# Sink set-up by DMA, start-up constants and the place of VectorE's last sum in a windowed-attention and highway kernel

## The chip, the cores and the metric

The kernel runs on one NeuronCore of one Trainium2 chip. A core has five engines that run side by side and meet only at semaphores: TensorE (PE; its weight loads are shown as PEld), VectorE (DVE), ScalarE (ACT), GpSimd (POOL) and SyncE (SP). Transfers between the chip's memory and the core's working memory (SBUF) run on 16 DMA engines; they are issued from GpSimd's queue and from SP's. TensorE writes its results to a second memory, PSUM. The metric is the device time of one launch in microseconds (us); lower is better.

## The reference

```python
scores = scale * np.matmul(q, k.transpose(0, 1, 3, 2))
is_sink = pos[None, :] < int(n_sink)
rel = pos[:, None] - pos[None, :]
in_window = (rel >= 0) & (rel < int(window))
scores = np.where(is_sink | in_window, scores, -1000000000.0)
scores = scores - np.max(scores, axis=-1, keepdims=True)
a = np.exp(scores)
a = a / (np.sum(a, axis=-1, keepdims=True) + 1e-09)
attn = np.matmul(a, v)
x = attn.transpose(0, 2, 1, 3).reshape(B * S, H * D)
Hh = np.maximum(x @ w_h, 0.0)
T = 1.0 / (1.0 + np.exp(-(x @ w_t + b_t)))
out = T * Hh + (1.0 - T) * x
```

q, k and v are (4, 8, 768, 64) in float32: 4 batches, 8 heads, 768 positions, 64 values a head. A query sees the 128 positions up to its own (the window) and the first 4 positions of its batch (the sink). The attention output, 3072 rows of 512, goes through a highway layer with two 512 x 512 weights.

## The kernel before

The 3072 rows are 24 blocks of 128 (NB = 24), six to a batch (NSC = 6). Block n = 6b + c is block c of batch b. With a window of 128, a block needs its own keys and those of the block before it; from c = 2 on it needs the sink as well.

One main loop (line 335) runs over i and works on several blocks at a time. In the pass of i it calls, in this order:

- `stage_sink(i)` for two blocks at once, where c is 2 or 4: scores of the sink keys (sk, L222) and their exponentials (es, L225).
- `stage_S(i+1)`: scores (sps, L242) and their exponentials on ScalarE (e, L245), in two halves.
- `stage_A(i)`: probabilities times values (av, L273), from c = 2 on also the sink's part (L279); then on VectorE the reciprocal of the row sums (rec, L286) and the scaled output (xh, L288).
- `stage_T(i+2)`: transposes of q and k into one PSUM tile (tp, L182 and L184), copied by ScalarE (qT, L187) and VectorE (kT, L188).
- `load` and `load_v` of block i+10 (q, k and v, cast to half precision on the way; L84, L85 and L92).
- `stage_mask(i+1)` on VectorE (L258).
- `stage_Mt(i-1)`: the first weight (tps, L307 and L309) and tanh on ScalarE (u, L312).
- `stage_X(i)`: xh transposed (xtp, L297) and copied by ScalarE (xT, L299).
- `stage_sink_setup` where c = 0: VectorE copies the batch's four sink keys into a block-diagonal tile (ks, L198); TensorE spreads the sink values over the partitions by a matmul with a selection matrix (vps, L203); VectorE multiplies the result by a block mask (vs, L207).
- `stage_Mh(i-1)`: the second weight (hps, L321), then on VectorE dd (L324), ee (L327) and otok (L330), and the output transfer from SP (L332).

The sigmoid is done as a tanh. The exponentials carry a common factor of 1.9, and the values have a column of 2.0 behind each head's 64 values, so that rec comes out of the same matmul as the output.

What sets the order: inside `manual_schedule` each engine that is named issues its instructions in the order in which the program emits them. In the main loop those are TensorE, VectorE and ScalarE; GpSimd and SP are placed there by the planner. A first region (line 106) names GpSimd alone and holds the first loads, the two weights and the making of `ident`, `mask` and `bdm`. How the instructions of one region fall among those of the same engine outside it is the planner's choice.

PSUM: tp, sk, tps and hps share one ring of two buffers (`m_ps`), so each of them waits until the tile two places earlier has been read. av, vps and xtp share a single buffer (`av_ps`). The scores have two (`s_ps`).

SBUF: eight buffers each for q and k as loaded, a ring of 11 tiles for v (`v_ring`), all of them set to 2.0 in full on VectorE before the first load (L104). All constants are written ahead of the main loop: `mask0` and `mask1` (L141 to L145), the bias row (L151, L155), `sel` (L159, L161) and the zeroed ks tiles (L167).

Of the kernel before, what the change touches and what calls it, by code (L numbers as in the profile page):

```python
# [21 lines left out]
def kernel(  # L22
# [18 lines left out]
    nc = tc.nc  # L41
# [25 lines left out]
    r_pool = ctx.enter_context(tc.tile_pool(name="p_r", bufs=3))  # L67
    x_pool = ctx.enter_context(tc.tile_pool(name="p_x", bufs=4))
    td_pool = ctx.enter_context(tc.tile_pool(name="p_td", bufs=3))
# [23 lines left out]


    ebias = const.tile([P, 1], FP32, tag="ebias")
    nc.vector.memset(ebias, _EXP_BIAS)
    wh_sb = const.tile([P, NOC, DM], FP16, tag="wh")
    wt_sb = const.tile([P, NOC, DM], FP16, tag="wt")
    ident = const.tile([P, P], FP16, tag="ident")
    mask = const.tile([P, 2, P], FP16, tag="mask", name="mask")  # L100
    nc.vector.memset(ident, 1.0)
    nc.vector.memset(mask, 1.0)
    for vt in v_ring:
        nc.vector.memset(vt, 2.0)  # L104

    with tc.manual_schedule(engines={ENG.Pool}):
        load(0)
        nc.gpsimd.affine_select(
            out=ident, in_=ident, compare_op=ALU.is_equal, fill=0.0,
            base=0, pattern=[[-1, P]], channel_multiplier=1)  # L110
        load_v(0)
        load(1)

        nc.gpsimd.affine_select(
            out=mask[:, 1, :], in_=mask[:, 1, :], compare_op=ALU.is_ge, fill=0.0,
            base=0, pattern=[[1, P]], channel_multiplier=-1)
# [8 lines left out]
        nc.gpsimd.dma_start(out=wh_sb, in_=moe_w_h.rearrange("(kc p) of -> p kc of", p=P))  # L125
        load_v(3)
        bdm = const.tile([P, H], FP32, tag="bdm")
        nc.gpsimd.memset(bdm, 1.0)
        bdm3 = bdm.rearrange("p (a b) -> p a b", b=2)
        nc.gpsimd.affine_select(  # L130
            out=bdm3, in_=bdm3, compare_op=ALU.is_ge, fill=0.0,
            base=0, pattern=[[-32, NHP], [-4, 2]], channel_multiplier=1)
        nc.gpsimd.affine_select(
            out=bdm3, in_=bdm3, compare_op=ALU.is_ge, fill=0.0,
            base=NSINK - 1, pattern=[[32, NHP], [4, 2]], channel_multiplier=-1)
        for n in range(4, AHEAD):
            load(n)
            load_v(n)

    mask0 = const.tile([P, P], FP16, tag="mask0", name="mask0")  # L140
    nc.vector.tensor_copy(out=mask0, in_=mask[:, 1, :])  # L141
    nc.vector.memset(mask0[0:NSINK, :], 1.0)
    mask1 = const.tile([P, 2, P], FP16, tag="mask1", name="mask1")
    nc.vector.tensor_copy(out=mask1, in_=mask)
    nc.vector.memset(mask1[0:NSINK, 0, :], 1.0)  # L145

# [7 lines left out]
    nc.vector.memset(ones_row[0:1, :], 1.0)  # L154
    nc.vector.tensor_scalar_mul(bt16[0:1, :], bt32, 0.5)  # L155


    sel = const.tile([P, NHP, 32], FP16, tag="sel")
    nc.vector.memset(sel, 0.0)  # L159
    for hh in range(2):  # L160
        nc.vector.tensor_copy(  # L161
            out=sel[:, :, 4 * hh:4 * hh + NSINK],
            in_=ident[:, 0:NSINK].unsqueeze(1).to_broadcast([P, NHP, NSINK]))
    ks_bd = []
    for i in range(2):
        t = const.tile([P, NHP * 160], FP16, tag=f"ks{i}", name=f"ks{i}")
        nc.vector.memset(t, 0.0)  # L167
        ks_bd.append(t)


    qkT = {}
    e_of = {}
    es_of = {}
    vs_of = {}
    xh_of = {}
    xT_of = {}

    def stage_T(n):
# [7 lines left out]
        kT = qkT_pool.tile([P, NHP, P], FP16, tag="kT", name="kT")  # L186
        nc.scalar.copy(out=qT, in_=tp[:, 0:NHP, :])  # L187
        nc.vector.tensor_copy(out=kT, in_=tp[:, NHP:2 * NHP, :])  # L188
        qkT[n] = (qT, kT)

    def stage_sink_setup(b):

        _, kT = qkT[b * NSC]
        ks = ks_bd[b % 2]
        ks3 = ks.rearrange("p (a b) -> p a b", b=160)
        for hh in range(2):
            rows = slice(64 * hh, 64 * hh + 64)
            nc.vector.tensor_copy(out=ks3[rows, :, 4 * hh:4 * hh + NSINK],  # L198
                                  in_=kT[rows, :, 0:NSINK])
# [5 lines left out]
        vs = es_pool.tile([P, 2, 4, 65], FP16, tag="vs", name="vs")  # L205
        for g in range(2):
            nc.vector.tensor_tensor(  # L207
                out=vs[:, g, :, :],
                in0=vps[:, g, 0:260].rearrange("p (h e) -> p h e", e=65),
                in1=bdm[:, 4 * g:4 * g + 4].unsqueeze(2).to_broadcast([P, 4, 65]),  # L210
                op=ALU.mult)
        vs_of[b] = vs

# [48 lines left out]
    def stage_A(n):  # L262
# [4 lines left out]
        for g in range(2):  # L267
# [10 lines left out]
            if c >= 2:  # L278
                nc.tensor.matmul(  # L279
                    av[:, g, :, 0:65], lhsT=es_of[n][:, c % 2, :],  # L280
                    rhs=vs_of[b][:, g, :, :], start=False, stop=True,
                    skip_group_check=True)
# [3 lines left out]
        nc.vector.reciprocal(out=rec.unsqueeze(2), in_=avh[:, :, 64:65])  # L286
        xh = x_pool.tile([P, H, D], FP16, tag="xh", name="xh")
        nc.vector.tensor_tensor(  # L288
# [26 lines left out]
    def stage_Mh(n):  # L315
        xT = xT_of.pop(n)
        xh = xh_of.pop(n).rearrange("p h d -> p (h d)")
# [9 lines left out]
        nc.vector.scalar_tensor_tensor(out=ee, in0=u, scalar=1.0, in1=dd,  # L327
                                       op0=ALU.add, op1=ALU.mult)
        otok = o_pool.tile([P, DM], FP32, tag="otok", name="otok")
        nc.vector.scalar_tensor_tensor(out=otok, in0=xh, scalar=2.0, in1=ee,  # L330
# [3 lines left out]
    with tc.manual_schedule(engines={ENG.PE, ENG.DVE, ENG.Activation}):  # L334
        for i in range(-2, NB + 1):
            s = i + 1
# [15 lines left out]
            if 0 <= i < NB:  # L352
                stage_X(i)
            if 0 <= i < NB and i % NSC == 0:
                stage_sink_setup(i // NSC)
            if 0 <= i - 1 < NB:
# [36 lines left out]
```

## Time and profile before

| what | us |
|---|---|
| median of 13 runs | 140.56 |
| lowest and highest run | 140.0 and 141.48 |
| the profiled execution | 141.32 |
| its span | 139.6 |
| busy in the span: TensorE, VectorE | 114.6, 117.3 |
| busy in the span: ScalarE, GpSimd | 90.5, 66.2 |
| first transposes of q and of k start | 5.0 and 6.64 |
| first scores (L242) start | 10.75 |
| last otok (L330) starts | 135.56 |

The page has the span in 40 equal slices; each digit is the busy share of a slice in tenths, and PEclk is the clock that TensorE was granted:

```profile
PE   0206779989999889999999699999996999999730
DVE  6895466769988999899898999898989998999590
ACT  3015961868776957987867497778768678874310
POOL 6999776599987988886748260000000000000000
PEclk9999999999999999999999999999999999999995
```

In a timeline row stand the start, the time taken, the engine, the line, the operation, the tile written and the tiles read, the shapes and the count; in brackets the engine's idle time ahead of it and what ended that. An engine with a letter q behind it (SPq) is that engine's queue.

### The profile page before, as it was taken

Reading aid. Unit: us, or ns where it says so; the run is one execution under the profiler, and the core shown is the slowest. Engines: PE = TensorE matmul, PEld = TensorE weight load, DVE = VectorE, ACT = ScalarE, POOL = GpSimd, SP = SyncE. Lnnn points to the kernel's source line nnn. Section 1 sums busy time; section 2 is a strip of 40 time slices with the busy share of each in tenths; the row PEclk is TensorE's granted clock in tenths of the full one; section 3 lists DMA queues with packets and bytes.
Section 4 is the critical chain, followed back from the end, with each engine's and each line's share of the span. In section 5 each row is a group of like instructions: output and inputs, shape, how many; then the busy total and the mean of one; then the engine's idle time right before and its main releaser. Section 6 shows DMA issues by size and latency. Waiting matters only on the chain.

```text
span 139.6 us, 3303 instructions
## 1 busy us (share of the span) xinstructions
PE 114.6 (82%) x1312; PEld 74.0 (53%) x1312; DVE 117.3 (84%) x235; ACT 90.5 (65%) x129; POOL 66.2 (47%) x84
## 2 busy tenths in 40 slices
PE   0206779989999889999999699999996999999730
PEld 0105656646754464766565367657653665675300
DVE  6895466769988999899898999898989998999590
ACT  3015961868776957987867497778768678874310
POOL 6999776599987988886748260000000000000000
PEclk9999999999999999999999999999999999999995
DMA  0999999999999999999999969221011021101111
GB/s 7 108 128 127 159 186 161 151 183 155 189 185 168 202 198 158 200 200 189 190 147 148 186 52 162 84 77 73 6 75 75 0 80 75 60 20 75 75 75 75
DMA packets 79408, 16.98 MB, mean 122 GB/s; under 512 B 75297, under 2 KB 76321, under 8 KB 79394
## 3 DMA queue, kind: packets, MB, share of 16 engines
q0 software_dynamic: 75936, 10.49, 111.8%
q1 hardware_dynamic: 3458, 6.30, 12.4%
q8 instruction: 10, 0.16, 0.5%
q14 instruction: 4, 0.03, 0.1%
HBM read 20.97 MB, written 6.29 MB: 195 GB/s over the span
## 4 chain that ended last, share of the span: by engine, by line
DVE 33%; PE 29%; DMA 13%; ACT 9%; issue 7%; POOL 6%; DVEq 0%; POOLq 0%
PE hps L321 11%; DMA ksd<-in_k_dram 7%; DVE ee L327 6%; DVE otok L330 6%; DMA wt_sb<-in_moe_w_t_dram 6%; DVE dd L324 6%; ACT e L245 6%; DVE e L258 5%; DVE xh L288 5%; PE tps L309 4%; PE xtp L297 3%; PE av L273 3%; DVE kT L188 3%; POOL qsd L84 3%; PE sk L222 2%
## 5 line engine op out<-in xcount | busy, mean ns | idle before, releaser
L245 ACT ACTIVATE e<-sps,ebias 128x1024 f16<-128x1024 f32 (+1 forms) x48 | 47.4, 1039 | 17.0 <-PE sps L242 13.0
L258 DVE TENSOR_TENSOR e<-e,mask 128x1024 f16<-128x1024 f16 (+1 forms) x48 | 28.7, 638 | 0.0
L92 POOL DMA_DIRECT2D v<-in_v_dram x24 | 21.6, 903 | 8.6 <-PE tp L182 5.8
L309 PE MATMUL tps<-wt_sb,xT 128*128 128x512 f16 x96 | 25.3, 388 | 0.0
L273 PE MATMUL av<-v,e 128*128 128x112 f16 x352 | 24.5, 219 | 0.7 <-DVE vs L207 0.7
L321 PE MATMUL hps<-wh_sb,xT 128*128 128x512 f16 x96 | 24.6, 378 | 0.6
L84 POOL DMA_DIRECT2D qsd<-in_q_dram x24 | 21.5, 896 | 6.9 <-DMA wt_sb<-in_moe_w_t_dram 1.5
L273 PEld LDWEIGHTS <-e 128*128 128x128 f16 x352 | 20.4, 100 | 4.0 <-DVE vs L207 1.0
L85 POOL DMA_DIRECT2D ksd<-in_k_dram x24 | 21.4, 892 | 2.0 <-DMA wh_sb<-in_moe_w_h_dram 1.2
L312 ACT ACTIVATE u<-tps 128x512 f16<-128x512 f32 x24 | 14.4, 600 | 9.6 <-PE tps L309 9.6
L324 DVE SCALAR_TENSOR_TENSOR dd<-hps,xh 128x512 f16<-128x512 f32 x24 | 16.5, 688 | 3.7 <-PE hps L321 3.7
L187 ACT COPY qT<-tp 128x512 f16<-128x512 f16 x24 | 14.0, 585 | 8.5 <-PE tp L184 8.5
L242 PE MATMUL sps<-qT,kT 64*128 64x128 f16 x352 | 15.2, 227 | 4.3 <-DVE kT L188 3.7
L327 DVE SCALAR_TENSOR_TENSOR ee<-u,dd 128x512 f16<-128x512 f16 x24 | 16.6, 692 | 2.5
L330 DVE SCALAR_TENSOR_TENSOR otok<-xh,ee 128x512 f32<-128x512 f16 x24 | 16.6, 692 | 0.8
L288 DVE TENSOR_TENSOR xh<-av,rec 128x512 f16<-128x512 f32 x24 | 16.6, 692 | 0.8
L242 PEld LDWEIGHTS <-kT 64*128 64x128 f16 x352 | 10.7, 98 | 11.7 <-issue 6.8
L188 DVE COPY kT<-tp 128x512 f16<-128x512 f16 x24 | 10.0, 419 | 6.2 <-ACT qT L187 6.2
L299 ACT COPY xT<-xtp 128x512 f16<-128x512 f16 x24 | 14.0, 582 | 1.4 <-PE xtp L297 0.9
L182 PE MATMUL tp<-ident,qsd 128*128 128x128 f16 x96 | 10.2, 235 | 5.2 <-DMA qsd<-in_q_dram 5.2
L309 PEld LDWEIGHTS <-xT 128*128 128x128 f16 x96 | 9.6, 100 | 9.1 <-issue 0.8
L297 PEld LDWEIGHTS <-xh 128*128 128x128 f16 x96 | 6.2, 100 | 13.6 <-DVE xh L288 11.5
(45 smaller groups left out, 107.0 us busy)
## 6 DMA issues: line engine op xcount, KB each, us to landing
out_dram<-otok SPq DMA_DIRECT2D x24, 256.0 KB, 3.0
qsd<-in_q_dram POOLq DMA_DIRECT2D x24, 128.0 KB, 6.9
ksd<-in_k_dram POOLq DMA_DIRECT2D x24, 128.0 KB, 7.0
v<-in_v_dram POOLq DMA_DIRECT2D x24, 128.0 KB, 7.5
wt_sb<-in_moe_w_t_dram POOLq DMA_DIRECT2D x1, 512.0 KB, 8.2
wh_sb<-in_moe_w_h_dram POOLq DMA_DIRECT2D x1, 512.0 KB, 9.9
bt<-in_moe_b_t_dram SPq DMA_DIRECT2D x1, 2.0 KB
```

What stands on the lines that cost most here:

```text
L84: nc.gpsimd.dma_start(out=qsd, in_=q[b, :, rows, :].transpose([1, 0, 2]))
L92: nc.gpsimd.dma_start(out=vt[:, :, 0:D], in_=v[b, :, rows, :].transpose([1, 0, 2]))
L242: nc.tensor.matmul(sps[:, hh, o:o + P], lhsT=kk[rows, hp, :], rhs=qT[rows, hp, :], start=True, stop=True)
L245: nc.scalar.activation(out=e.rearrange("p a b c d -> p a (b c d)"), in_=sps[:, :, 0:2 * np_ * P], func=AF.Exp, bias=ebias, scale=SCALE)
L258: nc.vector.tensor_tensor(out=ev, in0=ev, in1=m.unsqueeze(1).to_broadcast([P, 4, np_ * P]), op=ALU.mult)
L273: nc.tensor.matmul(av[:, g, 2 * hl + hh, 0:_AVN], lhsT=es[g][:, hh, hl, pc, :], rhs=vt[:, 65 * h:65 * h + _AVN], start=first, stop=False, ...
L288: nc.vector.tensor_tensor(out=xh, in0=avh[:, :, 0:D], in1=rec.unsqueeze(2).to_broadcast([P, H, D]), op=ALU.mult)
L309: nc.tensor.matmul(tps, lhsT=xT[:, kc, :], rhs=wt_sb[:, kc, :], start=False, stop=(kc == NOC - 1))
L321: nc.tensor.matmul(hps, lhsT=xT[:, kc, :], rhs=wh_sb[:, kc, :], start=(kc == 0), stop=(kc == NOC - 1))
L324: nc.vector.scalar_tensor_tensor(out=dd, in0=hps, scalar=0.0, in1=xh, op0=ALU.max, op1=ALU.subtract)
L327: nc.vector.scalar_tensor_tensor(out=ee, in0=u, scalar=1.0, in1=dd, op0=ALU.add, op1=ALU.mult)
L330: nc.vector.scalar_tensor_tensor(out=otok, in0=xh, scalar=2.0, in1=ee, op0=ALU.mult, op1=ALU.add)
```

## The change

It has two parts.

The first is at the start and in the sink set-up:

- `stage_sink_setup` no longer computes. Two DMAs from SP copy the sink keys out of kT into the block-diagonal tile, and eight DMAs copy the sink values, one head each, out of the v tile into a zeroed tile `vs_bd` (two of them, taken in turn by batches). `sel`, `bdm`, vps and vs are gone. It is called right behind the kT copy of a batch's first block, so two passes earlier than before.
- Of the v tiles only the column behind each head's values and the tail are written by memset. The first three are done ahead of everything, the others in the main loop (`init_v`), in front of their load.
- `mask0`, `mask1` and the scaled bias row are made in the pass of i = -2, behind the kT copy of block 0 (`late_constants`).
- Loads from block 3's v on are issued out of the main loop's first pass, no longer in GpSimd's hand-ordered region.
- In the pass of i = -2, ahead of the first transposes, TensorE runs eight matmuls of 128 x 512 on a zeroed tile (`warm_up(8)`); nobody reads their result.

The second is the order on VectorE: otok and the output transfer become `stage_out`, which is called for block i-2 between rec and xh of block i; ee is kept until then, and the pool of xh and xT has five buffers for four. The main loop has one pass more.

```diff
-    for vt in v_ring:
-        nc.vector.memset(vt, 2.0)
+    warm = const.tile([P, DM], FP16, tag="warm")
+    nc.vector.memset(warm, 0.0)
...
+    def init_v(vt):
+        nc.vector.memset(vt[:, 0:H * 65].rearrange("p (h e) -> p h e", e=65)[:, :, D:D + 1], 2.0)
+        nc.vector.memset(vt[:, H * 65:VW], 0.0)
+    for vt in v_ring[0:3]:
+        init_v(vt)
...
         nc.gpsimd.dma_start(out=wh_sb, in_=moe_w_h.rearrange("(kc p) of -> p kc of", p=P))
-        load_v(3)
-        bdm = const.tile([P, H], FP32, tag="bdm")
...
-        for n in range(4, AHEAD):
-            load(n)
-            load_v(n)
...
+    def warm_up(n):
+        w = m_ps.tile([P, DM], FP32, tag="m", name="wps")
+        for _ in range(n):
+            nc.tensor.matmul(w, lhsT=warm[:, 0:P], rhs=warm, start=True, stop=True)
...
     def stage_sink_setup(b):
         _, kT = qkT[b * NSC]
-        ks = ks_bd[b % 2]
-        ks3 = ks.rearrange("p (a b) -> p a b", b=160)
+        ks3 = ks_bd[b % 2].rearrange("p (a b) -> p a b", b=160)
         for hh in range(2):
             rows = slice(64 * hh, 64 * hh + 64)
-            nc.vector.tensor_copy(out=ks3[rows, :, 4 * hh:4 * hh + NSINK],
-                                  in_=kT[rows, :, 0:NSINK])
-        vps = av_ps.tile([P, 2, 512], FP32, tag="av", name="vps")
+            nc.sync.dma_start(out=ks3[rows, :, 4 * hh:4 * hh + NSINK],
+                              in_=kT[rows, :, 0:NSINK])
         vt = v_ring[(b * NSC) % NV]
-        for g in range(2):
-            nc.tensor.matmul(vps[:, g, 0:260], lhsT=sel.rearrange("p a b -> p (a b)"),
-                             rhs=vt[:, g * 260:(g + 1) * 260], start=True, stop=True)
...
+        for h in range(H):
+            r = 32 * (h // 2) + 4 * (h % 2)
+            nc.sync.dma_start(out=vs_bd[b % 2][r:r + NSINK, h // 4, h % 4, :],
+                              in_=vt[0:NSINK, 65 * h:65 * h + 65])
...
+    def stage_out(n):
+        xh = xh_of.pop(n).rearrange("p h d -> p (h d)")
+        ee = ee_of.pop(n)
         otok = o_pool.tile([P, DM], FP32, tag="otok", name="otok")
...
-        for i in range(-2, NB + 1):
+        for i in range(-2, NB + 2):
...
             if 0 <= i < NB:
                 stage_A(i)
+            if 0 <= i - 2 < NB:
+                stage_out(i - 2)
+            if 0 <= i < NB:
+                stage_xh(i)
+            if i == -2:
+                warm_up(8)
             if i + 2 < NB:
                 stage_T(i + 2)
-            if i + 2 + AHEAD < NB:
-                load(i + 2 + AHEAD)
-                load_v(i + 2 + AHEAD)
+                stage_T_k(i + 2)
+                if (i + 2) % NSC == 0:
+                    stage_sink_setup((i + 2) // NSC)
+            if i == -2:
+                late_constants()
+            for n in ([i + 2 + AHEAD] if i > -2 else range(3, AHEAD + 1)):
+                if n < NB:
+                    if n > 3:
+                        load(n)
+                    if 3 <= n < NV:
+                        init_v(v_ring[n])
+                    load_v(n)
```

`stage_T_k` is the kT copy, and `stage_xh` the line of xh, each cut out of the function that held it.

More of the change, by code (lines that the diff above doesn't have):

```diff
@@ L7 @@
 from concourse._compat import with_exitstack
-from concourse.masks import make_identity
 FP16 = mybir.dt.float16
@@ L125 @@
         nc.gpsimd.dma_start(out=wh_sb, in_=moe_w_h.rearrange("(kc p) of -> p kc of", p=P))
-        load_v(3)
-        bdm = const.tile([P, H], FP32, tag="bdm")
[L128 to L135, printed above, removed]
-        for n in range(4, AHEAD):
-            load(n)
-            load_v(n)
[L140 to L145, printed above, removed]
     bt32 = const.tile([1, DM], FP32, tag="bt32")
@@ L154 @@
     nc.vector.memset(ones_row[0:1, :], 1.0)
[L155 to L164, printed above, removed]
+    mask0 = const.tile([P, P], FP16, tag="mask0", name="mask0")
+    mask1 = const.tile([P, 2, P], FP16, tag="mask1", name="mask1")
+    ks_bd, vs_bd = [], []
     for i in range(2):
@@ L168, with late_constants @@
         ks_bd.append(t)
+        t = const.tile([P, 2, 4, 65], FP16, tag=f"vs{i}", name=f"vs{i}")
+        nc.vector.memset(t, 0.0)
+        vs_bd.append(t)
+    def warm_up(n):
+        w = m_ps.tile([P, DM], FP32, tag="m", name="wps")
+        for _ in range(n):
+            nc.tensor.matmul(w, lhsT=warm[:, 0:P], rhs=warm, start=True, stop=True)
+    def late_constants():
+        nc.vector.tensor_copy(out=mask0, in_=mask[:, 1, :])
+        nc.vector.memset(mask0[0:NSINK, :], 1.0)
+        nc.vector.tensor_copy(out=mask1, in_=mask)
+        nc.vector.memset(mask1[0:NSINK, 0, :], 1.0)
+        nc.vector.tensor_scalar_mul(bt16[0:1, :], bt32, 0.5)
     qkT = {}
@@ L173 @@
     es_of = {}
-    vs_of = {}
+    av_of = {}
+    ee_of = {}
+    kc_of = {}
     xh_of = {}
@@ L280, in stage_A @@
                     av[:, g, :, 0:65], lhsT=es_of[n][:, c % 2, :],
-                    rhs=vs_of[b][:, g, :, :], start=False, stop=True,
+                    rhs=vs_bd[b % 2][:, g, :, :], start=False, stop=True,
                     skip_group_check=True)
@@ L286, in stage_A, with stage_xh @@
         nc.vector.reciprocal(out=rec.unsqueeze(2), in_=avh[:, :, 64:65])
+        av_of[n] = (avh, rec)
+    def stage_xh(n):
+        avh, rec = av_of.pop(n)
         xh = x_pool.tile([P, H, D], FP16, tag="xh", name="xh")
@@ L353 @@
                 stage_X(i)
-            if 0 <= i < NB and i % NSC == 0:
-                stage_sink_setup(i // NSC)
             if 0 <= i - 1 < NB:
```

26 lines of the change are left out of this document (11 added, 15 removed).

## The prediction

> **What bounds the kernel now.** I read the page's span and chain lines first, then the busy time by pass of the main loop, cut at the starts of the hps matmuls (L321).
>
> ```profile
> span 139.6 us, 3303 instructions
> ...
> DVE 33%; PE 29%; DMA 13%; ACT 9%; issue 7%; POOL 6%; DVEq 0%; POOLq 0%
> ```
>
> ```profile
> 44.18:49.65 5.47, 4.23 (x50) 2.46 (x48) 4.85 (x10) 4.37 (x7) 4.97 (x6) 1.00 2.24 184
> 49.65:54.25 4.60, 4.32 (x55) 2.67 (x53) 4.40 (x12) 3.16 (x4) 3.79 (x5) 1.00 2.25 190
> 54.25:59.24 4.99, 4.90 (x65) 3.48 (x63) 4.42 (x9) 3.87 (x7) 4.36 (x5) 1.00 2.22 189
> 59.24:63.79 4.55, 4.55 (x55) 2.86 (x55) 4.38 (x9) 3.67 (x6) 3.81 (x5) 1.00 2.26 190
> ...
> 68.78:73.30 4.52, 4.34 (x48) 2.65 (x48) 4.35 (x9) 3.12 (x6) 2.52 (x4) 1.00 1.70 154
> ```
>
> After the stretch, its length and a comma stand the busy us of TensorE, weight loads, VectorE, ScalarE and GpSimd. The stretches run from the hps of one pass to that of the next; 44.18 to 73.30 is one batch, six stretches, 29.1 us. The first holds stage_sink_setup (it ends at the hps of pass i=6); the one of 4.99, and the one left out, hold stage_sink. VectorE and TensorE are both nearly full, so the chain (VectorE 33%, TensorE 29%) cannot say what a cheaper VectorE is worth. An ordinary pass, cut from the timeline, and one line of the waits say it:
>
> ```profile
> 60.20 0.62 PE L242 MATMUL sps<-qT,kT 64*128 64x128 f16 x16
> ...
> 60.69 2.12 ACT L245 ACTIVATE e<-sps,ebias 128x1024 f16<-128x1024 f32 x2 [0.65 <-ACT xT L299]
> ...
> 61.78 0.39 PE L182 MATMUL tp<-ident,qsd 128*128 128x128 f16 x4
> ...
> 62.44 0.20 DVE L286 RECIPROCAL rec<-av 128x8 f32<-128x8 f32 x1
> ...
> 62.67 0.69 DVE L288 TENSOR_TENSOR xh<-av,rec 128x512 f16<-128x512 f32 x1
> 62.70 0.58 ACT L187 COPY qT<-tp 128x512 f16<-128x512 f16 x1
> 63.31 0.42 DVE L188 COPY kT<-tp 128x512 f16<-128x512 f16 x1
> ...
> 63.79 1.02 PE L321 MATMUL hps<-wh_sb,xT 128*128 128x512 f16 x4
> ```
>
> ```profile
> DVE kT L188 <- ACT qT L187: 6.2, 10, 1.6
> ```
>
> The loop closes through **ScalarE**. From sps to the start of e 0.49; e and qT run to 63.28; kT, which waits for qT (ten times, by the last row), runs from 63.31 to 63.73; and hps, which takes the PSUM buffer that kT frees, starts 0.06 later. That is 3.59 from sps to hps; from hps (59.24) to sps 0.96; together 4.55, the pass. VectorE's xh ends at 63.36, so VectorE runs level with this loop.
>
> At the start, transfers bound. Issues from the timeline, then landing times from the DMA view (KB, us from issue) in order of issue: k of block 3 (issued 11.84), wh (12.70), the v of 15.40, k of block 4 (19.05):
>
> ```profile
> 10.35 0.35 DVE L188 COPY kT<-tp 128x512 f16<-128x512 f16 x1
> ...
> 11.84 0.94 POOL L85 DMA_DIRECT2D ksd<-in_k_dram  x1
> ...
> 12.70 0.83 POOL L125 DMA_DIRECT2D wh_sb<-in_moe_w_h_dram  x1
> ...
> 14.37 0.98 POOL L92 DMA_DIRECT2D v<-in_v_dram  x1
> ...
> 15.40 1.00 POOL L92 DMA_DIRECT2D v<-in_v_dram  x1
> ...
> 18.16 0.91 POOL L84 DMA_DIRECT2D qsd<-in_q_dram  x1 [1.53 <-DMA wt_sb<-in_moe_w_t_dram]
> 19.05 0.89 POOL L85 DMA_DIRECT2D ksd<-in_k_dram  x1
> ...
> 28.59 0.40 PE L184 MATMUL tp<-ident,ksd 128*128 128x128 f16 x4 [0.40 <-DMA ksd<-in_k_dram]
> ...
> 30.13 1.03 PE L321 MATMUL hps<-wh_sb,xT 128*128 128x512 f16 x4
> ```
>
> ```profile
> ksd<-in_k_dram POOLq DMA_DIRECT2D x1, 128.0 KB, 8.2
> wh_sb<-in_moe_w_h_dram POOLq DMA_DIRECT2D x1, 512.0 KB, 9.9
> v<-in_v_dram POOLq DMA_DIRECT2D x1, 128.0 KB, 11.5
> ksd<-in_k_dram POOLq DMA_DIRECT2D x1, 128.0 KB, 9.5
> ```
>
> So k of block 3 lands at 20.0, wh at 22.6, and k of block 4 at 28.55, where TensorE waits for it. Ahead of block 4's q the queue held two v transfers (14.37 and 15.40, the latter landing at 26.9). They come after block 3's v, in the gaps between the bdm instructions, where the program asks for block 4's q and k; I read them as those of blocks 8 and 9, which the planner pulled forward. Block 4's q (18.16) then waited for wt, eight transfers ahead of it.
>
> **The change, part by part.** *Constants off block 0.* kT of block 0 can start when its transposes end, near 7.3 (row of 6.65 below) instead of 10.35: 3.1 us. What is late next is the transfers: k of block 3 at 20.0, wh at 22.6, k of block 4. The 3.1 us turn into idle time ahead of block 3, and I count them as nothing. What does count is the order of loads. bdm goes, and the v slots of blocks 8 and 9 are initialised inside the hand-ordered loop, behind block 0, so I take it that block 3's v and block 4's q and k follow wh directly. They then stand at the places of 14.37 and 15.40, with as many transfers ahead, and block 4's k lands at 26.9, **1.6 earlier**. From its transposes to hps of that pass (28.59 to 30.13) nothing changes.
>
> *Sink DMAs.* Ten small transfers per batch: two of 64 x 4 pieces of 8 bytes, eight of 4 rows of 130 bytes, 544 pieces.
>
> ```profile
> q0 software_dynamic: 75936, 10.49, 111.8%
> ```
>
> ```profile
> out_dram<-otok SPq DMA_DIRECT2D x1, 256.0 KB, 5.3
> ```
>
> 75936 packets in 74 loads are about a thousand each, and loads go out 0.89 apart (18.16, 19.05): 544 pieces are worth 0.47 by count, nothing by bytes. I take 0.35, nearer the count, because the loads too are made of small packets. It delays block 4's k: 1.6 - 0.35 = **1.25** early (1.1 to 1.6 between the two ends). They are issued on SP when kT of blocks 0, 6, 12 and 18 is there. An out transfer beside the loads took 5.3 (second row); two such rounds for ten transfers are 11 us, from 7.4 to 18, and the first stage_sink cannot come before wh at 22.6. The other batches leave four passes, over 18 us. Behind them on SP stand only the out transfers, which have four otok buffers. On TensorE their semaphores are waited for ahead of the sink matmuls, with the pass's av behind them; no row shows it. The ends are nothing and one stall of 6.8/16 = 0.42 per batch (first row below). I take 0.1, nearer to nothing since all have landed: 3 x 0.1 = **+0.3**.
>
> *Setup off VectorE and TensorE.*
>
> ```profile
> PEld L242 <- issue: 6.8, 16, 0.6
> ```
>
> ```profile
> 49.79 0.34 DVE L198 COPY ks<-kT 64x16 f16<-64x16 f16 x2
> ...
> 50.14 0.76 DVE L207 TENSOR_TENSOR vs<-vps,bdm 128x260 f16<-128x260 f32 x2
> ```
>
> These 1.1 us of VectorE (49.79 to 50.90) lie in the stretch of 5.47 and the next. What is late next is the ScalarE loop, 4.55. In three batches 5.47 becomes 4.57 (with the 0.02 below) and 4.60 becomes 4.57: 0.93 x 3 = **2.8**.
>
> *Order on VectorE.* From rec to xh (62.64 to 62.67) there is a gap of 0.03; kT, which does not need xh, starts 0.05 before xh ends. Breaking the dependent pairs rec-xh and ee-otok saves about 0.11 each, 0.23 of VectorE a pass. But rec also needs av, and with otok gone from in front of it rec is ready first. Where it did wait for av it started 0.25 after the next stage's first matmul; 0.21 is the smallest lag seen (second pair):
>
> ```profile
> 15.04 0.63 PE L182 MATMUL tp<-ident,qsd 128*128 128x128 f16 x4
> ...
> 15.29 0.21 DVE L286 RECIPROCAL rec<-av 128x8 f32<-128x8 f32 x1 [1.22 <-PE av L273]
> ```
>
> ```profile
> 125.01 0.38 PE L307 MATMUL tps<-bt,ones_row 128*128 128x512 f16 x1
> ...
> 125.22 0.20 DVE L286 RECIPROCAL rec<-av 128x8 f32<-128x8 f32 x1
> ```
>
> So rec moves from 62.44 to 61.78 + 0.21 = 61.99; after it come otok and xh, and kT starts 0.12 + 0.61 + 0.61 later, at 63.33 instead of 63.31. An ordinary pass pays 0.02, and gains nothing: ten of them, **+0.2**. The last pass of a batch (4.52; half a block of e, so ScalarE has room) goes to about 4.40: 3 x 0.12 = **0.35** gained. In the last block but one there is no tp to cover the move: rec at 125.22 already starts with av, so xh moves by otok's 0.61 less 0.11; the following pass gives 0.23 back: **+0.27**.
>
> *Warm-up.* Eight matmuls of 512 columns at the early rate:
>
> ```profile
> 6.65 0.61 PE L184 MATMUL tp<-ident,ksd 128*128 128x128 f16 x4 [1.03 <-DMA ksd<-in_k_dram]
> ...
> 22.61 1.74 PE L309 MATMUL tps<-wt_sb,xT 128*128 128x512 f16 x4
> ```
>
> 1.74/4 = 0.43 each, 3.5 us from about 1.4 to 4.9; k of block 0, at 6.65, covers it. Four such matmuls take 1.03 later (30.13), though the granted clock reads 1.00 throughout: TensorE is slow at first. If it is quick at block 3, it has hps and sk (0.96 + 4.99 - 4.55 = 1.4), sps and av (60.20 to 61.78) left after wh at 22.6, and is ready for block 4 at 25.6, before k at 27.25. If it is slow all the way from 20.0, tp takes 0.6, tps 2.2, xtp and hps 2.2, and sk, sps and av an estimated 3.4: ready at 28.4, 1.1 after k.
>
> The Trainium skill (TensorE: Matmul & The Clock Gate, "The HAM clock gate") says that about 3.4 us of activity release the clock and an idle window as long throttles it again. By it the idle stretch ahead of block 3 can undo the warm-up, which is the rival "slow again". The rows of 22.61 and 30.13 agree that there are two rates; no run here shows the throttling back.
>
> **Sum**, on the profiled execution's 141.32 (its span and 1.7 around it, unchanged): -1.25 - 2.8 - 0.35 + 0.3 + 0.2 + 0.27 = -3.6, so 137.7. That execution lies 0.76 above the median of 140.56; the median after is **137.0**.
>
> **The rivals.** *Full start-up gain*: the 3.1 us count whole because the loads come still earlier: 1.85 more, 135.1. Against it: k of block 3 and wh stand where they stood. *VectorE bounds everywhere*: 0.23 on some 20 passes more, and the 0.2 not paid: 132.2. The ten waits of kT for qT speak against it. *Slow again*: the 1.1 above and 0.2 more for small transfers: 138.3. For it speaks the idle stretch of some 3 us. *It doesn't do what it says*: the planner still puts later v loads in front, and each batch stalls TensorE by 0.42: 1.25 + 3 x 0.32 lost, 139.2. *Slower*: rec, whose place is between av and xh, does not start when av ends. Every 0.1 us by which it comes later than 61.99 moves xh, kT and hps by 0.1 in some 18 passes, because otok's 0.61 now stands behind it. From 0.2 the gain of 3.6 is spent; half-way to today's 62.44 it costs 4.1, 141.1. The two rec pairs above speak against it.
>
> **How the numbers follow.** Forecast 0.55, full start-up 0.12, VectorE everywhere 0.05, slow again 0.13, not as said 0.08, slower 0.07. The range 135.1 to 139.2 leaves out the third and the last, and some of the others through mis-sized terms: 0.8. Faster by over 0.3% (about what a measurement of this kernel can tell from no change): 0.87; within, 0.06, from the weaker ends of the last two; slower, 0.07.
>
> **What would show it.** kT of block 0 near 7.4; TensorE idle ahead of block 3's k; block 4's q issued right after block 3's v, its k landing near 27; the stretch with the setup at 4.6; ordinary ones still 4.55 and 4.99, with kT waiting for qT; xh of block 22 later. It is wrong if ordinary stretches change by over 0.1, or if block 4's k transposes come before 26 or after 28.

## The result, and the profile after

The kernel after takes 136.06 us (median of 11 runs, 135.18 to 136.95), the kernel before 140.54 (48 runs on the same chips, 139.72 to 141.54): a ratio of 0.968, 95% interval 0.965 to 0.971. The forecast was 137.0 with a range of 135.1 to 139.2. The profiled execution took 136.67, of which 135.0 are its span; before, 141.32 and 139.6.

From the page of the kernel after: the granted clock in 40 slices and the chain that ended last.

```profile
PEclk9965775799999999999999999999999999999999
...
PE 62%; DVE 8%; ACT 8%; POOL 7%; issue 7%; DMA 6%; POOLq 0%; DVEq 0%
```

TensorE now has 62% of the chain where it had 29%, and VectorE 8% where it had 33%. That looks as if the bound had moved to TensorE; an experiment below shows that an ordinary pass leaves TensorE room. What the kernel gained is read from the stretches between the hps of one pass and that of the next. Columns as in the prediction's table: the stretch, its length, busy us of TensorE, weight loads, VectorE, ScalarE and GpSimd.

```profile
42.71:47.26 4.55, 4.00 (x48) 2.27 (x46) 3.81 (x9) 3.95 (x7) 3.81 (x5) 1.00 2.18 184
47.26:51.80 4.54, 4.34 (x53) 2.67 (x53) 4.25 (x9) 3.55 (x6) 3.54 (x5) 1.00 2.47 154
51.80:56.80 5.00, 5.00 (x64) 3.40 (x64) 4.26 (x9) 3.83 (x7) 4.93 (x7) 1.00 2.36 150
56.80:61.34 4.54, 4.54 (x56) 2.87 (x55) 4.24 (x9) 3.66 (x6) 4.32 (x6) 1.00 2.03 215
...
66.34:70.62 4.28, 4.28 (x49) 2.64 (x48) 4.18 (x9) 2.88 (x6) 2.56 (x4) 1.00 2.20 194
117.17:122.02 4.85, 4.46 (x56) 2.91 (x55) 4.11 (x8) 3.88 (x6) 0.00 (x0) 1.00 0.12 47
122.02:126.19 4.17, 3.36 (x34) 2.02 (x32) 3.62 (x7) 1.19 (x3) 0.00 (x0) 1.00 0.16 63
```

The first five are the counterparts of the five rows before. The stretch that held the sink set-up fell from 5.47 to 4.55, the one behind it from 4.60 to 4.54, the last of a batch from 4.52 to 4.28; the ordinary ones stand at 4.54 and 5.00, unmoved. At the end of the kernel, stretches that took 4.41 and 4.41 take 4.85 and 4.17 (before, hps starts there at 122.03, 126.44 and 130.85).

An ordinary pass in the timeline after, and the waits of kT in the whole kernel (us in total, times, longest):

```profile
59.34 0.39 PE L183 MATMUL tp<-ident,qsd 128*128 128x128 f16 x4
...
59.54 0.21 DVE L282 RECIPROCAL rec<-av 128x8 f32<-128x8 f32 x1 [0.19 <-PE av L275]
59.66 0.65 DVE L335 SCALAR_TENSOR_TENSOR otok<-xh,ee 128x512 f32<-128x512 f16 x1
60.23 0.69 DVE L288 TENSOR_TENSOR xh<-av,rec 128x512 f16<-128x512 f32 x1
60.25 0.58 ACT L188 COPY qT<-tp 128x512 f16<-128x512 f16 x1
60.87 0.42 DVE L194 COPY kT<-tp 128x512 f16<-128x512 f16 x1
```

```profile
DVE kT L194 <- ACT qT L188: 9.4, 10, 3.2
```

rec starts 0.20 behind the first tp matmul, as forecast (0.21), and VectorE waits 0.19 for it; before, it started 0.66 behind tp (62.44 and 61.78), without a wait. Then otok and xh run, and kT starts 0.04 after qT has ended (60.25 + 0.58 = 60.83): the same neighbour as before. VectorE arrives level with it: kT starts 0.05 before xh ends. Without otok's 0.57 (59.66 to 60.23), kT could by an estimate from these rows have started near 60.3, ahead of qT's end: otok moved into time in which kT would have waited for ScalarE.

The row of waits says less. None of its ten lies in an ordinary pass: four are at the start, six, of 0.18 to 0.20, in the stretches of the set-up and behind it. In the kernel before too, four of the ten were at the start and six (0.39 to 0.40) in passes with stage_sink. What bounds an ordinary pass is left to the experiments.

The start, TensorE alone, and the time from issue to landing of wh (issued 12.88) and of block 4's k (issued 15.37):

```profile
4.83 0.40 PE L183 MATMUL tp<-ident,qsd 128*128 128x128 f16 x4
...
15.85 1.17 PE L269 MATMUL av<-v,e 128*128 128x112 f16 x16
18.89 0.61 PE L183 MATMUL tp<-ident,qsd 128*128 128x128 f16 x4 [1.87 <-DMA qsd<-in_q_dram]
19.73 0.61 PE L185 MATMUL tp<-ident,ksd 128*128 128x128 f16 x4 [0.23 <-DMA ksd<-in_k_dram]
...
22.68 1.91 PE L321 MATMUL hps<-wh_sb,xT 128*128 128x512 f16 x4
...
27.11 0.39 PE L185 MATMUL tp<-ident,ksd 128*128 128x128 f16 x4
```

```profile
wh_sb<-in_moe_w_h_dram POOLq DMA_DIRECT2D x1, 512.0 KB, 9.3
```

```profile
ksd<-in_k_dram POOLq DMA_DIRECT2D x1, 128.0 KB, 9.7
```

Block 4's k landed at 25.1, not at 28.55 as before, and its transposes came at 27.11 without waiting for it: TensorE was late. The four transposes of block 3's k took 0.61 where 0.39 is the quick time, and hps 1.91 where it takes 1.02 later. The hps of the pass that holds block 4's transposes came at 28.89; before, at 30.13.

By the starts of hps, the span's 4.6 are made up of 1.24 at the start (30.13 to 28.89), 0.92 + 0.06 in each of three set-ups and 0.23 (4.50 to 4.27) in each of three last passes of a batch, together 3.63, and 0.20 given back at the end (0.44 - 0.24).

### The profile page after: what moved, and what is told of

Its sections match the earlier page's. It is cut to its first block, busy times and chain, and to the rows that moved or that the text cites. A ratio compares the mean times of both kernels' runs of the same rounds, so it can differ in the third digit from the quotient of the medians.

```text
span 135.0 us, 3379 instructions
## 1 busy us (share of the span) xinstructions
PE 118.2 (88%) x1312; PEld 73.0 (54%) x1312; DVE 105.4 (78%) x230; ACT 89.7 (66%) x129; POOL 65.9 (49%) x81
## 4 chain that ended last, share of the span: by engine, by line
PE 62%; DVE 8%; ACT 8%; POOL 7%; issue 7%; DMA 6%; POOLq 0%; DVEq 0%
PE hps L321 17%; PE av L269 11%; PE tps L309 10%; PE sps L238 6%; DMA ksd<-in_k_dram 6%; ACT e L241 5%; PE xtp L297 4%; PE sk L218 3%; PE tp L185 3%; PE tps L307 3%; PE av L275 3%; PE tp L183 2%; ACT qT L188 2%; POOL ksd L84 2%; POOL qsd L83 2%
## 5 line engine op out<-in xcount | busy, mean ns | idle before, releaser
L321 PE MATMUL hps<-wh_sb,xT 128*128 128x512 f16 x96 | 25.5, 388 | 1.3 <-DVE kT L194 1.3
L269 PE MATMUL av<-v,e 128*128 128x112 f16 x352 | 24.0, 215 | 0.1
L269 PEld LDWEIGHTS <-e 128*128 128x128 f16 x352 | 19.8, 98 | 3.3 <-DVE e L254 0.6
L335 DVE SCALAR_TENSOR_TENSOR otok<-xh,ee 128x512 f32<-128x512 f16 x24 | 15.8, 657 | 0.1
L309 PEld LDWEIGHTS <-xT 128*128 128x128 f16 x96 | 9.6, 100 | 9.1 <-issue 0.8
L321 PEld LDWEIGHTS <-xT 128*128 128x128 f16 x96 | 9.4, 99 | 9.5 <-issue 2.6
```

Of the source, the lines that this page charges most:

```text
L269: nc.tensor.matmul(av[:, g, 2 * hl + hh, 0:_AVN], lhsT=es[g][:, hh, hl, pc, :], rhs=vt[:, 65 * h:65 * h + _AVN], start=first, stop=False, ...
L309: nc.tensor.matmul(tps, lhsT=xT[:, kc, :], rhs=wt_sb[:, kc, :], start=False, stop=(kc == NOC - 1))
L321: nc.tensor.matmul(hps, lhsT=xT[:, kc, :], rhs=wh_sb[:, kc, :], start=(kc == 0), stop=(kc == NOC - 1))
```

## The experiments

The theory: an ordinary pass closes through ScalarE, so the change pays only where something else had been later (the set-up passes, the last pass of a batch, the start). The rivals: TensorE bounds the loop, as the chain now says, or VectorE does; and at the start, the early constants or the warm-up bring the gain, not the order of the loads.

### The parts alone

*Order undone*: the kernel after, with otok back at its old place.

```diff
-        for i in range(-2, NB + 2):
+        for i in range(-2, NB + 1):
...
-            if 0 <= i - 2 < NB:
-                stage_out(i - 2)
...
                 stage_Mh(i - 1)
+                stage_out(i - 1)
```

> The changed kernel with otok back behind ee (the second part undone). My theory (ScalarE's loop sets ordinary passes): stretches between hps starts stay 4.55 and 4.99; only the last stretch of a batch goes back from 4.27 to 4.50 (3 x 0.23), and the end gains back 0.2: some 0.5 us over the changed kernel, about 136.5 us, ratio to before 0.971. Rival (VectorE bounds every pass, so the order is most of the gain): 0.23 in 20 passes, 4.6 us over the changed kernel.

Measured: 136.93 (4 runs), ratio 0.973 (0.966 to 0.979). The last stretch of a batch, and the same stretch's VectorE:

```profile
38.02:42.52 4.50, 4.33 (x47) 2.64 (x47) 4.33 (x9) 3.10 (x6) 4.46 (x6) 1.00 2.03 209
```

```profile
39.88 0.69 DVE L327 SCALAR_TENSOR_TENSOR ee<-u,dd 128x512 f16<-128x512 f16 x1
40.60 0.69 DVE L335 SCALAR_TENSOR_TENSOR otok<-xh,ee 128x512 f32<-128x512 f16 x1
41.21 0.20 DVE L282 RECIPROCAL rec<-av 128x8 f32<-128x8 f32 x1
41.45 0.69 DVE L288 TENSOR_TENSOR xh<-av,rec 128x512 f16<-128x512 f32 x1
42.05 0.41 DVE L194 COPY kT<-tp 128x512 f16<-128x512 f16 x1
```

The same work in the kernel after:

```profile
68.20 0.69 DVE L327 SCALAR_TENSOR_TENSOR ee<-u,dd 128x512 f16<-128x512 f16 x1
68.86 0.21 DVE L282 RECIPROCAL rec<-av 128x8 f32<-128x8 f32 x1
68.98 0.65 DVE L335 SCALAR_TENSOR_TENSOR otok<-xh,ee 128x512 f32<-128x512 f16 x1
69.55 0.68 DVE L288 TENSOR_TENSOR xh<-av,rec 128x512 f16<-128x512 f32 x1
70.15 0.41 DVE L194 COPY kT<-tp 128x512 f16<-128x512 f16 x1
```

From the start of ee to that of kT it was 2.17 and is 1.95. Set side by side, the step behind ee shrinks from 0.72 to 0.66, the one behind rec from 0.24 to 0.12, and the one behind otok from 0.61 to 0.57: neighbours that do not need each other overlap. qT had ended at 69.89, so nothing else is late here, and the 0.22 is gained. All other stretches of this kernel are those of the kernel after (4.55 and 5.0), and its end has 4.41 and 4.41 again. By the stretches the order is thus worth 0.49 (3 x 0.23 - 0.20). The medians cannot show it: the intervals of this kernel and of the kernel after overlap, and in this trace the start is shorter by 0.41 (second hps at 28.48).

*Order alone*: the kernel before, with only `stage_out` and `stage_xh` cut out, otok placed between rec and xh, and the fifth buffer for xh and xT.

```diff
-        for i in range(-2, NB + 1):
+        for i in range(-2, NB + 2):
...
+            if 0 <= i - 2 < NB:
+                stage_out(i - 2)
+            if 0 <= i < NB:
+                stage_xh(i)
```

> The kernel before with the new place of otok alone. My theory: only stretches that VectorE bounds get shorter: the one with the sink set-up 5.47 to 5.24, the one behind it 4.61 to 4.55, the last of a batch 4.50 to 4.27, 0.5 a batch; the end loses 0.2; the rest unchanged: 1.3 us less than before, ratio 0.991. Rival (VectorE everywhere): 4.6 us less, ratio 0.967. Rival (xh late in every pass): over 1.

Measured: 139.25 (9 runs), ratio 0.991 (0.987 to 0.994). The first stretch with the sink set-up and the one behind it (4.74 here, 4.56 in the next batch):

```profile
43.95:49.23 5.28, 4.22 (x49) 2.45 (x47) 4.53 (x10) 4.41 (x7) 4.54 (x6) 1.00 2.22 184
49.23:53.97 4.74, 4.40 (x55) 2.67 (x53) 4.61 (x12) 3.11 (x4) 4.05 (x5) 1.00 2.24 188
```

The order takes 0.19 off the set-up stretch (5.47 to 5.28) and the 0.23 off the last one; ordinary stretches stay at 4.55 and 4.99, and block 4's k is transposed at 28.60, as before. The two parts do not add up simply: the order's 0.19 lies inside the 0.92 that the sink DMAs take off by themselves (with the order undone, above, the set-up stretch is 4.55).

*Sink set-up back on VectorE and TensorE*, the rest as after (bdm made on GpSimd behind wh's load, the call back in the pass of c = 0):

```diff
-            nc.sync.dma_start(out=ks3[rows, :, 4 * hh:4 * hh + NSINK],
-                              in_=kT[rows, :, 0:NSINK])
+            nc.vector.tensor_copy(out=ks3[rows, :, 4 * hh:4 * hh + NSINK],
+                                  in_=kT[rows, :, 0:NSINK])
...
+            nc.tensor.matmul(vps[:, g, 0:260], lhsT=sel.rearrange("p a b -> p (a b)"),
+                             rhs=vt[:, g * 260:(g + 1) * 260], start=True, stop=True)
...
+            nc.vector.tensor_tensor(
+                out=vs[:, g, :, :],
```

> The changed kernel with the sink set-up computed on VectorE and TensorE at its old place, bdm behind the weights. My theory: the stretch with the set-up goes from 4.55 to about 5.24 (5.47 less the 0.23 of the new order), the next up to 4.60: 0.7 x 3 = 2.1 us, and some 0.2 earlier landings without the small transfers; about 138.0 us, ratio 0.982. Rival (the small transfers cost as much as they save): time within 0.5 us of the changed kernel.

Measured: 138.61 (4 runs), ratio 0.988 (0.980 to 0.996).

```profile
41.67:46.95 5.28, 4.22 (x49) 2.46 (x47) 4.54 (x10) 4.41 (x7) 4.21 (x6) 1.00 2.27 186
46.95:51.54 4.59, 4.36 (x56) 2.67 (x54) 4.46 (x12) 3.12 (x4) 4.16 (x6) 1.00 2.22 186
```

5.28 against 4.55 and 4.59 against 4.54, three times over, is 2.3 of the 2.55 by which the medians differ; the start is not later (second hps at 27.86). The sink DMAs are the larger half of the change.

*Warm-up removed*: `warm_up(8)` becomes `pass`.

```diff
             if i == -2:
-                warm_up(8)
+                pass
```

> The changed kernel without the eight matmuls. My theory: TensorE is slow again when block 3's k lands, warmed up or not, so block 4's transposes of k start at 27.1 as in the changed kernel, plus or minus 0.3, and the time is the same within 0.4 us. Rival (the warm-up is what brought block 4 forward): block 4's transposes 1 us or more later, time 1 us more.

Measured: 137.10 (4 runs), ratio 0.976 (0.970 to 0.982), beside 0.968 (0.965 to 0.971) with it. The medians differ by 1.04, but the intervals overlap. In its trace block 4's k was transposed at 27.62, outside the 27.1 plus or minus 0.3 that I expected. wh landed at 23.9 there (22.2 after), though it was issued at the same time; hps waited 0.46 for it, and the hps of block 4's pass came 0.5 later, at 29.40. TensorE was no slower: the four tps matmuls of block 0 took 1.91 in both traces. Whether the warm-up is worth anything is not settled by these runs; what speaks against it stands under the hardware, below.

### The start

*Constants early*: v tiles set in full and `late_constants` called ahead of the loop, the loads' order as after.

```diff
-    for vt in v_ring[0:3]:
-        init_v(vt)
+    for vt in v_ring:
+        nc.vector.memset(vt, 2.0)
...
+    late_constants()
...
-            if i == -2:
-                late_constants()
```

> The changed kernel with the constants made ahead of the main loop again: all eleven v tiles set in full, mask0, mask1 and the bias row in front. Order of loads as in the changed kernel. My theory (3 us at block 0 become idle time ahead of block 3): kT of block 0 goes from 7.3 to some 10, but block 3's transposes stay at 19 to 20.5 and block 4's between 26 and 27.7; time within 0.6 us of the changed kernel, ratio 0.968 to 0.973. Rival (start-up gain counts whole): 2 to 3 us over the changed kernel, 138.5 or more.

Measured: 135.96 (4 runs), ratio 0.969 (0.965 to 0.973). In this kernel the kT of block 0, which the kernel after has at 7.30, comes 4.8 later:

```profile
12.06 0.40 DVE L196 COPY kT<-tp 128x512 f16<-128x512 f16 x1
```

The time is that of the kernel after. So taking the constants out of block 0's path brings nothing that the medians show. In the traces two things stand against each other. Block 3's transposes of q came at 21.31, later than the 20.5 at most that I expected (18.89 after), so the kernel after does turn part of the time into idle time ahead of block 3. But TensorE ran up to them without a gap here, they were quick (0.38), and the second hps came at 28.05, 0.84 earlier than in the trace after. wh (22.5) and block 4's k (25.2) landed about as they do there. No run separates the two.

*The v of blocks 8 and 9 ahead of block 4's q and k*, as the planner of the kernel before had them:

```diff
-    for vt in v_ring[0:3]:
+    for vt in v_ring[0:4] + v_ring[8:10]:
         init_v(vt)
...
+        load_v(3)
+        load_v(8)
+        load_v(9)
...
+                    if n in (3, 8, 9):
+                        continue
```

> The changed kernel with the v transfers of blocks 8 and 9 issued ahead of block 4's q and k, as in the kernel before. My theory (this order held block 4 back): its k lands two places later, at 27 to 28.5 instead of 25.0, its transposes of k start then instead of 26.1 to 27.6: 0.5 to 1.4 us over the changed kernel, about 136.9. Rival (the order is worth nothing, the rest of the start-up brought block 4 forward): same time as the changed kernel within 0.3.

Measured: 136.90 (4 runs), ratio 0.974 (0.971 to 0.978): 0.84 over the kernel after. TensorE waits for k again:

```profile
27.67 0.40 PE L188 MATMUL tp<-ident,ksd 128*128 128x128 f16 x4 [0.44 <-DMA ksd<-in_k_dram]
```

So the order of the loads counts at the start, but how much of it is not settled: the intervals just touch (0.971), and the second hps came at 29.21, 0.32 later than in the trace after and 0.92 earlier than before. k landed at 27.6 here, 2.5 later than in the kernel after, but 0.9 earlier than in the kernel before. That 0.9 I have not traced to a transfer; wh, issued within 0.25 in all thirteen kernels, lands between 22.2 and 23.9, so one trace of each cannot tell it from chance.

*TensorE kept quick*: eight more unread matmuls ahead of block 3, where TensorE had 1.87 of idle time.

```diff
-            if i == -2:
+            if i in (-2, 1):
                 warm_up(8)
```

> The changed kernel with eight more matmuls on the zeroed tile ahead of block 3's transposes. My theory (TensorE is slow after the idle stretch ahead of block 3, and that, not the landing of k at 25.0, sets block 4's transposes at 27.1): with the idle stretch filled TensorE stays quick, block 4's k transposes come at 25.1 to 26.3, 0.8 to 2 us less than the changed kernel, about 135.0, ratio 0.960. Rival (landings bind): no change; the eight matmuls at the slow rate take 3.4 us and could push block 3 back by 0.7.

Measured: 135.92 (6 runs), ratio 0.966 (0.962 to 0.970). Its start:

```profile
17.44 3.18 PE L159 MATMUL wps<-warm 128*128 128x512 f16 x8
...
22.30 1.04 PE L321 MATMUL hps<-wh_sb,xT 128*128 128x512 f16 x4
```

The mechanism is there: block 3's transposes of k in 0.39 (from 20.68), hps in 1.04, and the second hps at 27.30, 1.6 earlier than in the trace after. The medians differ by 0.14 only, inside the intervals. The reason is in the other traces. The wh weight landed (issue plus time to landing), the first two hps started, and the transposes of block 3's k took:

| kernel | wh | first hps | second hps | between | transposes |
|---|---|---|---|---|---|
| before | 22.6 | 24.41 | 30.13 | 5.72 | 0.63 |
| order alone | 22.7 | 24.06 | 30.13 | 6.07 | 0.63 |
| after | 22.2 | 22.68 | 28.89 | 6.21 | 0.61 |
| order undone | 22.9 | 23.39 | 28.48 | 5.09 | 0.61 |
| more on TensorE (below) | 23.2 | 23.61 | 28.77 | 5.16 | 0.61 |
| more on ScalarE (below) | 22.8 | 23.04 | 28.04 | 5.00 | 0.61 |
| more on VectorE (below) | 22.2 | 22.19 | 27.20 | 5.01 | 0.40 |
| TensorE kept quick | 22.3 | 22.30 | 27.30 | 5.00 | 0.39 |
| the same, other end (below) | 23.2 | 23.24 | 28.25 | 5.01 | 0.39 |
| set-up back on VectorE | 22.5 | 22.86 | 27.86 | 5.00 | 0.61 |
| no warm-up | 23.9 | 23.90 | 29.40 | 5.50 | 0.61 |
| constants early | 22.5 | 23.05 | 28.05 | 5.00 | 0.39 |
| v of 8 and 9 first | 22.9 | 23.39 | 29.21 | 5.82 | 0.61 |

Where TensorE is quick by the first hps and k is not late, the stretch from that hps to the second takes 5.0, as long as any other stretch with stage_sink: neither loads nor TensorE bind it. The five kernels whose start is that of the kernel after differ by 1.7 at the second hps (27.20 to 28.89), in part by when wh lands, in part by how long TensorE stays slow; the trace after is the slowest of them. The second kernel with the fillers has its second hps at 28.25, later than four of the kernels without them. The fillers had more to save in that one execution after than in most, and six runs within 1.6 us of one another cannot tell the rest from nothing. That last step is read from the table, not shown.

*The same, and xh of block 22 ahead of otok*, the version with the lowest median:

```diff
+            if i == NB - 2:
+                stage_xh(i)
             if 0 <= i - 2 < NB:
                 stage_out(i - 2)
-            if 0 <= i < NB:
+            if 0 <= i < NB and i != NB - 2:
                 stage_xh(i)
```

> The kernel b3_keep_quick with xh ahead of otok in the pass of block 22 alone, which has no transposes of q and k to cover otok. My theory: that stretch goes from 4.85 back to 4.41 with the last at 4.17, 0.4 us under b3_keep_quick, about 134.6, ratio 0.957. Rival: what is gained there is lost in the last pass, which goes to 4.6.

Measured: 135.85 (6 runs), ratio 0.964 (0.960 to 0.968). The end:

```profile
116.52:120.92 4.40, 4.40 (x56) 2.90 (x55) 3.62 (x7) 3.43 (x6) 0.00 (x0) 1.00 0.13 49
120.92:125.45 4.53, 3.57 (x35) 1.90 (x32) 4.14 (x8) 1.53 (x3) 0.00 (x0) 1.00 0.15 61
```

4.40 + 4.53 against 4.85 + 4.17: 0.09 gained, not 0.44. The otok that was passed is in the way one pass later. Against the kernel after the intervals overlap, so this version is not shown to be faster.

### What bounds an ordinary pass

Three kernels, each the kernel after with useless work on one engine, in every pass from block 4 (ScalarE: block 6) on; one run each. *ScalarE*, a copy ahead of qT:

```diff
+        if n >= 6:
+            nc.scalar.copy(out=junk[:, 0:P], in_=warm[:, 0:P])
         nc.scalar.copy(out=qT, in_=tp[:, 0:NHP, :])
```

> The changed kernel with one more ScalarE copy (128x128, SBUF to SBUF, of a tile nobody reads) ahead of qT, from block 6 on: some 0.25 to 0.36 us. My theory (the loop sps, e, qT, kT, hps closes through ScalarE): every stretch with transposes grows by all of it, 4.55 and 4.99 to 4.8 to 4.9 and 5.25 to 5.35. Rival (TensorE's own work sets the stretches; its chain share is 62%): ScalarE, busy 66%, has room, and they stay within 0.1.

```profile
56.66:61.35 4.69, 4.56 (x55) 2.87 (x55) 4.29 (x9) 3.83 (x7) 4.25 (x6) 1.00 1.99 224
61.35:66.53 5.18, 5.02 (x64) 3.40 (x64) 4.30 (x9) 4.27 (x8) 3.17 (x4) 1.00 2.08 204
```

```profile
65.22 0.30 ACT L190 COPY junk<-warm 128x128 f16<-128x128 f16 x1
65.41 0.60 ACT L191 COPY qT<-tp 128x512 f16<-128x512 f16 x1
```

The copy takes 0.30, but qT starts 0.19 after the copy's start, so 0.19 is what ScalarE's step grows by. The passes grow by 0.15 and 0.18: ScalarE's time goes into them almost whole. The last of a batch does not move (4.27).

*VectorE*, a memset of 0.27 behind ee:

```diff
+        if n >= 4:
+            nc.vector.memset(junk[:, 0:256], 1.0)
```

> The changed kernel with one more VectorE memset (128x256, 0.27, some 0.2 of it on the engine's way) between ee and rec, from block 4 on. My theory: rec waits for av by about 0.2 to 0.3, so ordinary stretches stay 4.55 and 4.99 within 0.05; only the last of a batch and the one after it may grow, by up to 0.2. Rival (VectorE bounds): all grow by 0.2.

```profile
55.11:59.66 4.55, 4.55 (x57) 2.87 (x56) 4.44 (x10) 3.67 (x6) 4.20 (x6) 1.00 2.45 176
...
64.65:69.08 4.43, 4.34 (x49) 2.64 (x48) 4.32 (x10) 3.03 (x6) 3.51 (x5) 1.00 2.19 191
```

VectorE's busy time rises, the ordinary passes (4.55, and 4.99 in the stretch left out) do not; the last of a batch does, by 0.15. It is the mirror image of the ScalarE kernel. The room is ahead of rec: in the pass of 55.11 the memset takes the whole wait of 0.19, and rec still starts 0.20 behind tp. Behind rec, where VectorE arrives level with qT, nothing was added.

*TensorE*, one more 128 x 512 matmul, its result overwritten by the next:

```diff
+        if n >= 4:
+            nc.tensor.matmul(tps, lhsT=ones_row, rhs=bt16, start=True, stop=True)
```

> The changed kernel with one more 128x512 matmul (0.216) ahead of the bias matmul of tps, from block 4 on; its result is overwritten. My theory: xtp waits for xh by some 0.1 and hps for kT by some 0.05, so half of it shows: 4.55 to 4.65, 4.99 to 5.1. Rival (TensorE alone sets the stretches): all of the 0.216, 4.77 and 5.21. Rival (TensorE has room): nothing.

```profile
56.68:61.23 4.55, 4.55 (x60) 3.04 (x57) 4.25 (x9) 3.67 (x6) 4.18 (x5) 1.00 2.14 201
```

Nothing moves (the stretch with stage_sink is 4.99 again), although TensorE was already shown busy for the whole of each stretch. My expectation that part of it would show was wrong. TensorE had room behind the "busy": in the pass of 4.54 xtp's weight load had 0.43 of idle time ahead of it, waiting for xh, and here it has 0.22; the kernel after first:

```profile
60.97 0.23 PEld L297 LDWEIGHTS <-xh 128*128 128x128 f16 x4 [0.43 <-DVE xh L288]
```

```profile
60.85 0.32 PEld L297 LDWEIGHTS <-xh 128*128 128x128 f16 x4 [0.22 <-DVE xh L288]
```

The chain's 62% for TensorE is where the chain passes, not what a shorter TensorE would save. The matmul stood between tp and hps, though, where TensorE has to wait. By the prediction's rows the loop itself holds 1.45 of TensorE (hps to sps 0.96, sps to e 0.49); work added there was not tried.

## Why the prediction was right

The forecast moved by 3.6, the medians by 4.5. Step by step:

- *Ordinary passes* were forecast at +0.02 each, all through ScalarE. They stayed at 4.55 and 4.99; the three kernels with more work show that ScalarE's time sets them, with room on VectorE ahead of rec and on TensorE behind tp. One ground given for it was misread: none of the ten waits of kT for qT, also held against "VectorE everywhere", lies in an ordinary pass. The 0.2 charged for ten of them was not paid.
- *Setup passes*: 0.93 three times was forecast, 0.98 came (0.92 + 0.06). With the old set-up put back, 0.78 of it is lost.
- *Last pass of a batch*: mis-sized, and the largest of the errors that the sum shows. The step "goes to about 4.40: 3 x 0.12" charged half of VectorE's 0.23; 0.23 came, three times. The forecast's own rule for an ordinary pass (rec 0.21 behind tp, then 0.12, 0.61 and 0.61) should have been put on this pass's rows: kT would start 1.55 behind tp. In the trace after it starts 70.15 - 68.66 (tp) = 1.49 behind, against 72.82 - 71.10 = 1.72 before. Most of the gain was to be had from rows of the kernel before.
- *Sink waits*: 0.1 a batch was charged, nothing came: the stretches with stage_sink are 5.00, those before were 4.99. The 0.35 for the small transfers at the start no run separates.
- *End*: +0.27 forecast, +0.20 in the trace; as forecast, xh of block 22 pays for otok in front of it and the next pass gives about half back.
- *Start*: 1.25 forecast and 1.24 in the trace, but not in the way forecast. Block 4's q was issued right behind block 3's v, as said; its k landed at 25.1, not near 27 (26.9 + 0.35). The forecast took the 11.5 from issue to landing over from the v of 15.40; in the ten kernels with this order block 4's k took 9.0 to 11.3 and landed between 25.0 and 26.7. Instead TensorE was late, the rival "slow again", which the forecast priced at 1.1: in the trace it made the first stretch 6.21 instead of 5.0. Two errors of opposite sign met: that 1.24 came out beside 1.25 is luck. In the medians, what the batches and the end leave over is 4.48 - 3.63 + 0.20 = 1.05.
- *Full start-up gain* and *VectorE everywhere* fell: block 0 later by 4.8 cost nothing that the medians show, and more work on VectorE, ahead of rec, cost an ordinary pass nothing. *Slower* fell with rec at 0.20 behind tp. *Not as said* fell: no later v stood in front, and no stall showed.

So 0.3 for the sink waits, 0.2 for the ordinary passes, 0.34 for the last pass, 0.14 for the set-up and 0.07 for the end were the forecast's excess of caution, 1.05 in all; the start, by the medians, gave 0.2 less than charged.

The Trainium skill (TensorE: Matmul & The Clock Gate, "HAM oscillation — how this bites in real kernels") gives as the rule for keeping the clock that TensorE has no idle gaps over about 3.4 us. The trace after shows less to be enough: the 16 matmuls of av at 15.85 are quick (1.17), and behind 1.87 of idle time the transposes at 18.89 are slow (0.61). A drop earlier in the same trace came behind a shorter one: the eight matmuls of block 0's scores at 7.78 are quick (0.40), and block 1's transposes at 8.51, behind 0.34 of idle time, are slow (0.61); gaps of 1.02 and 1.14 lie not far ahead of them. So the length of a single gap does not decide; how much idle time is little enough no run here tells.

## What to carry to other kernels

Put independent work into the place where an engine waits, not only where it is cheap: otok between rec and xh cost an ordinary pass nothing because VectorE would have waited there for qT. Do the sum for each kind of pass on its own rows, the short ones too; the gain of a cheaper engine lies where the usual bound is absent. A share of the chain, or an engine busy for a whole stretch, does not name the bound; a little useless work on each engine in turn tells more, in one run each, for the place in the pass where it is put.

## What the runs showed of the hardware

The warm-up is a lottery. The same eight matmuls, from 1.26 to about 4.8, were followed by quick transposes of block 0's q (0.40) in four of the ten kernels that have them, the one after among them, and by slow ones (0.61) in six. In two of the six the rate changed right behind: block 0's k took 0.40 there. And where block 0's q was quick, block 1's q was slow again (0.61) each time: at 8.5 to 8.7 in the kernel after, in the one with the memset on VectorE and in the version with the lowest median, and at 13.06, behind 5.78 of idle time, with the constants early. The Trainium skill (TensorE: Matmul & The Clock Gate, "The HAM clock gate") says that the window in which activity is counted runs freely, so that the warm-up ends at another point in each run; these traces agree.

The record of the granted clock does not always tell TensorE's rate. In the kernel before it reads 1.00 throughout, and in the one with TensorE kept quick it reads 1.00 from 3 to 30 us, yet in both the early matmuls are slow (tp in 0.63 at 21.34, and in 0.61 at 4.85). In the trace after it falls to 5 to 7 tenths in slices 3 to 8, in agreement with the durations. The durations are the safer witness.

Runs of one kernel scatter by up to 2.1 us (order undone: 135.66 to 137.72). After the second hps the stretches of the five kernels with the same start agree to 0.02 where their code is the same, so the scatter that the traces show comes from before it: wh was issued between 12.68 and 12.89 in them and landed between 22.2 and 23.2. Their second hps came at 28.28 on average, 0.61 ahead of the trace after, and that execution lies 0.61 above the kernel's median.

The ten small sink transfers of a batch, 544 pieces by the program, are issued over some 9 us (66.31 to 75.08 in the trace after), in the last stretch of a batch and the set-up stretch behind it. The last stretch takes 4.28 with them and 4.27 in the kernel with the set-up back on VectorE, which has none: no mark that can be measured. What they cost the loads at the start no run separates.
